# Moving an SBUF-to-SBUF transpose hop from the SyncE and ScalarE queues to GpSimd's queue

## The chip, the core and the metric

The kernel runs on one core of one Trainium2 chip. Five engines work from queues of their own: TensorE (PE), VectorE (DVE), ScalarE (ACT), GpSimd (POOL) and SyncE (SP). DMAs are begun by an instruction in the queue of SyncE, ScalarE or GpSimd and then carried by the core's 16 DMA engines. The metric is the device time of one execution, in microseconds; the median of two runs before the change is 1986.13 us (1984.96 to 1987.31).

## The reference

Two operators in a row, on an input of 8 batches x 3136 positions x 256 channels, float32:

```python
# 1: a filter along the sequence, by FFT
X = np.fft.rfft(x, axis=1)
Y = X * (filt_r + 1j * filt_i)[None]
x = np.fft.irfft(Y, n=x.shape[1], axis=1).astype(np.float32)
# 2: a gated feed-forward block
h = np.maximum(x @ w_in, 0.0)                      # 256 -> 1024
conv_out = sum(conv_w[k] * shifted(h, k) for k in range(3))   # along the sequence
out = (h * sigmoid(conv_out)) @ w_out              # 1024 -> 256
```

## The kernel before

The FFT of 3136 = 112 x 28 points is done as matrix products in stages. The first part of the kernel (the forward part, `NI` loop steps `i`) treats the eight batches as 8 x 14 = 112 pieces, each a pair of the 28 columns (`p` = 0 to 13). For a piece:

- `load` (L299): SyncE loads `x`, 112 partitions x 2 x 256 floats.
- `first` (L320): two matmuls with the table `s1` into a PSUM tile `ps`.
- `store_a` (L304): ScalarE copies `ps` to the SBUF tile `sa`.
- `turn` (L309), the hop: row 28r + g of `sa`, half j, goes to partition 14(2r + j) + p, place g, of the big tile `a_even` or `a_odd` (one for even batches, one for odd). What lay along partitions then lies along a row.
- `second` (L327): a matmul of one pair of columns of the whole `a` tile; it needs all 14 hops of its batch. Result in PSUM `pp`.
- `filt` (L337): three DVE products with the filter (`u`, and two halves of `v`), and on GpSimd z = u + v (L347).
- `third` (L349): two matmuls with `i1` into `ps`; `store_b` (L315): ScalarE copies to `sb` and begins the store to the DRAM tile `b_dram`.

In loop step `i` the order on each compute engine is as written: `load` for piece i+5, `filt` for i-18, `third` for i-20, `first` for i-1, `second` for i-17, the hop for i-2, then `store_b` and `store_a`. So hops are issued in steps 2 to 113, and the second stage begins in step 17. PE, ACT, DVE and POOL keep the written order (`manual_schedule`); SyncE's queue is put in order by a scheduler that knows what each DMA depends on. Between these, in the early steps, tables and filters are loaded, and the FFN weights, which come as 64-bit floats, are turned into 32-bit ones by DVE and GpSimd (`to_f32`, L157; `convert_weights`, L277; tile `ws`). Every engine's queue is served in order: an instruction that waits holds up all behind it.

The second part is the FFN (L428 on), with the last inverse stage of the next batch (`last_load`, `last_stage`, `last_out`, L199 to L225) put between its steps. The last stage of batch 0 runs in the last steps of the first part.

Number of buffers: `x` 7, `sa` 4, `sb` 4, `ws` 2. GpSimd's space for its DMA lists is `dynamic_dma_scratch_size=1024` bytes a partition. In each step the hop is eight DMAs of 28 rows of 1 KB, one for each half j and quarter r: six in SyncE's queue (`BY_SP = 6`), two in ScalarE's.

Of the kernel before, what the change touches and what calls it, by code (L numbers as in the profile page):

```python
# [9 lines left out]
F32 = mybir.dt.float32  # L10
# [10 lines left out]
D = 256  # L21
# [106 lines left out]
def tile_fft_filter_gated_ffn(  # L128
# [16 lines left out]
    nc = tc.nc  # L145
    B = x.shape[0]

    def hi_act(dst, src):
        nc.scalar.activation(dst, src, AF.Copy)  # L149
# [4 lines left out]
    def lo_pool(dst, src, hi):  # L154
        nc.gpsimd.tensor_tensor(out=dst, in0=src, in1=hi.bitcast(F32), op=ALU.subtract)  # L155

    def to_f32(dst, raw, e, m):  # L157


        v = nc.vector  # L160
        pairs = raw.rearrange("p (n t) -> p n t", t=2)
        low, high = pairs[:, :, 0].bitcast(U32), pairs[:, :, 1]
        v.tensor_scalar(e, high, 3, 0x3FFFFFF8, op0=ALU.logical_shift_left, op1=ALU.bitwise_and)
        yield
        v.tensor_scalar(m, high, 30, 30, op0=ALU.logical_shift_right, op1=ALU.logical_shift_left)
        yield
        v.tensor_tensor(out=e, in0=e, in1=m, op=ALU.bitwise_or)
        yield
        v.tensor_scalar(m, high, 27, 0xF, op0=ALU.logical_shift_right, op1=ALU.bitwise_and)
        yield  # L170
        v.scalar_tensor_tensor(out=dst, in0=m, scalar=7.0, in1=e.bitcast(F32), op0=ALU.is_ge, op1=ALU.mult)
        yield
        v.tensor_scalar(e, dst.bitcast(I32), 23, 23, op0=ALU.logical_shift_right, op1=ALU.logical_shift_left)
        yield
        v.scalar_tensor_tensor(out=e.bitcast(F32), in0=low, scalar=2.0**-52, in1=e.bitcast(F32), op0=ALU.mult, op1=ALU.mult)
        yield
        nc.gpsimd.tensor_tensor(out=dst, in0=dst, in1=e.bitcast(F32), op=ALU.add)
# [50 lines left out]
    xp = forward_pools.enter_context(tc.tile_pool(name="xp", bufs=2, side="right"))  # L228
    s1_sb = xp.tile([112, N2, 112], F32, name="s1_sb", bufs=1)
    a_sb = [xp.tile([112, G, D], F32, name="a_even", bufs=1)]  # L230
    with (
# [16 lines left out]
        rows = {}  # L248

        def load_filter(c):  # L250
            sl = slice(4 * c, 4 * c + 4)
            for t, src in ((t1_sb, fr), (t2_sb, fi)):
                nc.sync.dma_start(out=t[0:64, sl], in_=src[:, sl])
# [10 lines left out]
        def load_weights(k):  # L264
            raws[k] = raw = cv.tile([128, 2, 256], I32, name="raw")
            for part, src in enumerate((w_in, w_out)):
                nc.sync.dma_start(out=raw[:, part], in_=src[:, 256 * k:256 * k + 256])
# [9 lines left out]
        def convert_weights():  # L277

            for k in range(16):
                raw = raws.pop(k)  # L280
                em = cv.tile([128, 2, 256], I32, name="em", bufs=1)
                ws = cv.tile([128, 2, 128], F32, name="ws")
                yield from to_f32(ws.rearrange("p t n -> p (t n)"), raw.rearrange("p t n -> p (t n)"), em[:, 0], em[:, 1])
                yield
                parts = [[t.rearrange("p a b -> p (a b)")[:, 128 * k:128 * k + 128] for t in w] for w in (wi, wo)]
                for part, (wh, wl) in enumerate(parts):
                    hi_act(wh, ws[:, part])
                yield
                for part, (wh, wl) in enumerate(parts):
                    lo_pool(wl, ws[:, part], wh)  # L290
                    yield
                if k < 14:
                    load_weights(k + 2)
# [3 lines left out]
        psums = {}  # L297

        def load(b, p):  # L299
            r = xp.tile([112, 2, D], F32, name="x", bufs=7)  # L300
            nc.sync.dma_start(out=r, in_=x[b].rearrange("(p n) d -> p n d", n=N2)[:, 2 * p:2 * p + 2])
            rows["x", b, p] = r

        def store_a(b, p, ps):  # L304
            st = xp.tile([112, 2, D], F32, name="sa", bufs=4)
            nc.scalar.activation(st, ps, AF.Copy)  # L306
            rows["sa", b, p] = st

        def turn(engine, b, p, which):  # L309
            for q in which:  # L310
                j, r = divmod(q, 4)
                row = 14 * (2 * r + j) + p
                engine.dma_start(out=a_sb[b % 2][row:row + 1], in_=rows["sa", b, p][28 * r:28 * r + 28, j])  # L313

        def store_b(b, p, ps):  # L315
            st = fp.tile([112, 2, D], F32, name="sb", bufs=4)
            nc.scalar.activation(st, ps, AF.Copy)  # L317
            nc.scalar.dma_start(out=b_dram[b].rearrange("n (r g) d -> (n r) g d", g=G)[:, 2 * p:2 * p + 2], in_=st)

# [17 lines left out]
        def filt(b, p):  # L337


            pp, v = psums.pop((b, p)), turned[p % 2]  # L340
            sl = slice(2 * p, 2 * p + 2)
            u = fp.tile([120, 2, D], F32, name="u")
            nc.vector.tensor_mul(u, pp, t1_sb[:, sl])  # L343
            nc.vector.tensor_mul(v[64:120], pp[0:56], t2_sb[0:56, sl])  # L344
            nc.vector.tensor_mul(v[0:56], pp[64:120], t2_sb[64:120, sl])  # L345
            z = fp.tile([120, 2, D], F32, name="z", bufs=3)
            nc.gpsimd.tensor_tensor(out=z, in0=u, in1=v, op=ALU.add)  # L347
            parts["z", b, p] = z

        def third(b, p):  # L350
            z = parts.pop(("z", b, p))
            ps = fps.tile([112, 2, D], F32, name="ps")
            for j in range(2):
                nc.tensor.matmul(ps[:, j], lhsT=i1_sb[:, 2 * p + j], rhs=z[:, j], start=True, stop=True)  # L354
            return ps

        def at(i):
            return divmod(i, NP) if 0 <= i < NP * B else None
# [12 lines left out]
        with tc.manual_schedule(engines=COMPUTE):  # L371
            for i in range(NI):
                f, m = i, i - SKEW
                if i == done:
                    forward_pools.close()
                    yps.append(ctx.enter_context(tc.tile_pool(name="y_even", bufs=1, side="right", reuse_waits="tile")))
                    lp = ctx.enter_context(tc.tile_pool(name="lp", bufs=2, side="right", reuse_waits="tile"))
                if 1 <= i < 5:
                    nc.sync.dma_start(out=s1_sb[:, 4 * i + 8:4 * i + 12], in_=s1[:, 4 * i + 8:4 * i + 12])
                if (bp := at(f + 5)) and i:  # L380
                    load(*bp)
                if i == 6:
                    nc.sync.dma_start(out=s2_sb, in_=s2)
                    nc.sync.dma_start(out=s2s_sb, in_=s2s)
                    nc.sync.dma_start(out=m2_sb, in_=m2)
                if 12 <= i < 26 and i % 2 == 0:
                    sl = slice((i - 12) // 2 * 4, (i - 12) // 2 * 4 + 4)
                    load_filter(i // 2 - 6)
                    nc.sync.dma_start(out=i1_sb[:, sl], in_=i1[:, sl])
                if bp := at(m - 2):  # L390
                    filt(*bp)
                pt = third(*bp) if (bp := at(m - 4)) else None
                pf = first(*bp) if (bp := at(f - 1)) else None
                if bp := at(m - 1):
                    second(*bp)
                if bp := at(f - 2):
                    turn(nc.sync, *bp, range(BY_SP))
                    turn(nc.scalar, *bp, range(BY_SP, 8))
                    del rows["sa", bp[0], bp[1]]
                if pt is not None:  # L400
                    store_b(*at(m - 4), pt)
                if pf is not None:
                    store_a(*at(f - 1), pf)
                if 3 <= i < 16:
                    next(csteps, None)
                if i == 16:
                    load_weights(0)
                    load_weights(1)
                if i >= 22:
                    next(wsteps, None)  # L410
                    next(wsteps, None)
                if 16 <= i < 30 and i % 2 == 0:
                    copy_filter(i // 2 - 8)
                c = 2 * (i - done)
                if 0 <= c - 4 < N2:
                    last_out(0, c - 4)
                if 0 <= c - 2 < N2:
                    last_stage(0, c - 2, fps.tile([128, 512], F32, name="ps"))
                if 0 <= c < N2:
                    last_load(0, c)  # L420
# [107 lines left out]
                evacuate(*a)  # L528


BY_SP = 6
PLAG = 6
AVOID = (3, 4, 5, 6, 7)
COMPUTE = {mybir.EngineType.PE, mybir.EngineType.Activation, mybir.EngineType.DVE, mybir.EngineType.Pool}
# [38 lines left out]
```

## Time and profile before

| | us |
|---|---|
| median of the runs | 1986.13 |
| the profiled execution, its reported time | 1985.82 |
| its span, first to last instruction | 1983.9 |
| busy: PE / DVE / ACT / POOL | 1611.3 / 1322.9 / 1193.2 / 689.5 |
| forward part, to the first FFN matmul | 796 |
| FFN part | 1188 |
| mean granted TensorE clock | 0.891 |

In the profile, L313 is a line of the kernel before. SPq and ACTq are the DMA-issuing queues of SyncE and ScalarE; the time of an issue is the time in which that queue does nothing else. `a_even<-sa` is a DMA from `sa` to `a_even`. A group's row ends with the idle time before its instructions and who ended it. The reported time is 1.9 us more than the span.

### The profile page before, as it was taken

The numbers are of one execution on the slowest core, as the hardware profiler recorded it, in microseconds if no ns is written. First come the engines' busy times: TensorE is split into PE (matmuls) and PEld (weight loads), VectorE is DVE, ScalarE is ACT, GpSimd is POOL, SyncE is SP. The second block draws the span as 40 slices with busy tenths as digits, with TensorE's granted clock in tenths as the row PEclk, the third lists the DMA queues.
The fourth block names the chain that finished last, engine by engine and source line by source line (L and its number), as shares of the span: only waits on it lengthen the run. The fifth ranks groups of instructions, "written<-read, shape, count | busy, mean of one in ns | idle before, by whom it ended". The sixth has DMA issues, their size and how long they took to land.

```text
span 1983.9 us, 27237 instructions
## 1 busy us (share of the span) xinstructions
PE 1611.3 (81%) x9424; PEld 1382.6 (70%) x9424; DVE 1322.9 (67%) x2021; ACT 1193.2 (60%) x2178; POOL 689.5 (35%) x648
## 2 busy tenths in 40 slices
PE   4165647475645538999999999999999999999999
PEld 2032324243323326899999999999999999999998
DVE  0043526253544428788888888888888888888887
ACT  1122112121212114888888888888888888888887
POOL 0021313122212213344444444444444444444444
PEclk6576778676877769999999999999999999999999
DMA  4455444344444435011111111111111111110101
GB/s 122 99 136 138 109 112 114 105 120 111 121 109 118 105 89 155 29 43 53 37 43 44 47 43 48 42 43 43 47 43 44 46 42 43 48 42 21 37 19 38
DMA packets 127005, 141.22 MB, mean 71 GB/s; under 512 B 19899, under 2 KB 100884, under 8 KB 126868
## 3 DMA queue, kind: packets, MB, share of 16 engines
q1 hardware_dynamic: 103123, 107.35, 19.2%
q10 hardware_dynamic: 23744, 32.13, 6.1%
q8 instruction: 75, 1.23, 0.3%
q14 instruction: 63, 0.51, 0.1%
HBM read 62.34 MB, written 51.38 MB: 57 GB/s over the span
## 4 chain that ended last, share of the span: by engine, by line
PE 59%; DVE 2%; SPq 1%; DMA 1%; ACT 1%; issue 1%; ACTq 0%; POOL 0%; DVEq 0%; POOLq 0%
PE ps_h L181 9%; PE ps_h L182 9%; PE ps_h L180 9%; PE po L479 9%; PE po L481 9%; PE po L480 9%; PE ps_h L218 4%; SPq L313 1%; DVE y L152 1%; DMA a_odd<-sa 1%; ACT y L149 0%; DVE v L344 0%; DVE u L343 0%; PE ps L354 0%; PE pp L331 0%
## 5 line engine op out<-in xcount | busy, mean ns | idle before, releaser
L155 POOL TENSOR_TENSOR g<-t,g 128x448 fp32r<-128x448 f32 x448 | 517.3, 1155 | 667.8 <-ACT g L149 264.1
L479 PE MATMUL po<-wo,g 128*128 128x256 f32 x1568 | 441.5, 282 | 0.0
L481 PE MATMUL po<-wo,g 128*128 128x256 f32 x1568 | 433.8, 277 | 0.0
L480 PE MATMUL po<-wo,g 128*128 128x256 f32 x1568 | 433.4, 276 | 0.0
L453 DVE SCALAR_TENSOR_TENSOR t<-ps_h,cw,t 128x448 f32<-128x448 f32 x448 | 305.7, 682 | 83.3 <-ACT t L448 73.0
L343 DVE TENSOR_TENSOR u<-pp,t_sb 120x512 f32<-120x512 f32 x112 | 77.5, 692 | 417.6 <-PE pp L331 325.7
L181 PE MATMUL ps_h<-y,wi 128*128 128x450 f32 x896 | 330.7, 369 | 4.2 <-DVE y L152 4.2
L180 PE MATMUL ps_h<-y,wi 128*128 128x450 f32 x896 | 329.2, 367 | 3.5 <-ACT y L149 2.1
L182 PE MATMUL ps_h<-y,wi 128*128 128x450 f32 x896 | 329.0, 367 | 0.0
L454 DVE SCALAR_TENSOR_TENSOR t<-ps_h,cw,t 128x448 f32<-128x448 f32 x448 | 306.5, 684 | 16.0
L448 ACT ACTIVATE t<-ps_h,cw 128x448 f32<-128x448 f32 x448 | 284.8, 636 | 42.9 <-ACT ps_h L446 2.2
L347 POOL TENSOR_TENSOR z<-u,v 120x512 f32<-120x512 f32 x112 | 145.5, 1301 | 449.2 <-DVE v L345 382.9
L306 ACT ACTIVATE sa<-ps 112x512 f32<-112x512 f32 x112 | 66.9, 597 | 389.6 <-DMA a_even<-sa 174.3
L479 PEld LDWEIGHTS po<-wo,g 128*128 128x128 f32 x1568 | 294.8, 188 | 7.1
L480 PEld LDWEIGHTS po<-wo,g 128*128 128x128 f32 x1568 | 294.3, 188 | 5.7
L481 PEld LDWEIGHTS po<-wo,g 128*128 128x128 f32 x1568 | 294.5, 188 | 0.0
L459 DVE TENSOR_TENSOR t<-ps_h,t 128x448 f32<-128x448 f32 x448 | 275.4, 615 | 0.1
L446 ACT ACTIVATE ps_h<-ps_h 128x450 f32<-128x450 f32 x448 | 251.8, 562 | 32.1 <-PE ps_h L182 27.5
L458 ACT ACTIVATE t<-t 128x448 f32<-128x448 f32 x448 | 255.0, 569 | 11.9 <-DVE t L454 10.8
L149 ACT ACTIVATE g<-t 128x448 fp32r<-128x448 f32 x448 | 254.7, 568 | 0.2 <-DVE t L459 0.2
L324 PE MATMUL ps<-x,s_sb 112*112 112x256 f32 x448 | 162.9, 502 | 86.7 <-ACT sb L317 41.7
L354 PE MATMUL ps<-z,i_sb 120*112 120x256 f32 x448 | 145.9, 456 | 94.8 <-ACT sa L306 51.7
(57 smaller groups left out, 1776.8 us busy)
## 6 DMA issues: line engine op xcount, KB each, us to landing
x<-in_x SPq DMA_DIRECT2D x112, 224.0 KB
b_dram<-sb ACTq DMA_DIRECT2D x112, 224.0 KB
br<-b_dram SPq DMA_DIRECT2D x112, 224.0 KB
out<-ot SPq DMA_DIRECT2D x27, 896.0 KB
a_even<-sa SPq DMA_DIRECT2D x336, 28.0 KB
a_odd<-sa SPq DMA_DIRECT2D x336, 28.0 KB
a_even<-sa ACTq DMA_DIRECT2D x112, 28.0 KB
a_odd<-sa ACTq DMA_DIRECT2D x112, 28.0 KB
```

The lines of the kernel that those rows point to most:

```text
L155: nc.gpsimd.tensor_tensor(out=dst, in0=src, in1=hi.bitcast(F32), op=ALU.subtract)
L180: nc.tensor.matmul(ps, lhsT=wh, rhs=rh, start=start, stop=False, **kw)
L181: nc.tensor.matmul(ps, lhsT=wh, rhs=rl, start=False, stop=False, **kw)
L182: nc.tensor.matmul(ps, lhsT=wl, rhs=rh, start=False, stop=stop, **kw)
L448: nc.scalar.activation(t, h[:, 1:SUB + 1], AF.Copy, scale=cw[:, 1, f:f + 1])
L453: nc.vector.scalar_tensor_tensor(out=t, in0=h[:, 0:SUB], scalar=cw[:, 0, f:f + 1], in1=t, op0=ALU.mult, op1=ALU.add)
L454: nc.vector.scalar_tensor_tensor(out=t, in0=h[:, 2:SUB + 2], scalar=cw[:, 2, f:f + 1], in1=t, op0=ALU.mult, op1=ALU.add)
L458: nc.scalar.activation(t, t, AF.Sigmoid)
L459: nc.vector.tensor_mul(t, h[:, 1:SUB + 1], t)
L479: nc.tensor.matmul(o, lhsT=gh[:, sl], rhs=wo[0][:, f], start=first, stop=False, skip_group_check=True)
L480: nc.tensor.matmul(o, lhsT=gh[:, sl], rhs=wo[1][:, f], start=False, stop=False, skip_group_check=True)
L481: nc.tensor.matmul(o, lhsT=gl[:, sl], rhs=wo[0][:, f], start=False, stop=last, skip_group_check=True)
```

## The change

The hop is begun by GpSimd, in the same place of the loop step, as two DMAs, one for each half j. Each takes all 112 rows of its half of `sa`; its destination is four partitions, 28 apart. To make room for GpSimd's DMA lists, which grow from 1024 to 8192 bytes a partition, `x` has 6 buffers, `sa` and `sb` 3, `ws` 1. The FFN's code is the same.

```diff
-                ws = cv.tile([128, 2, 128], F32, name="ws")
+                ws = cv.tile([128, 2, 128], F32, name="ws", bufs=1)
...
-            r = xp.tile([112, 2, D], F32, name="x", bufs=7)
+            r = xp.tile([112, 2, D], F32, name="x", bufs=6)
...
-            st = xp.tile([112, 2, D], F32, name="sa", bufs=4)
+            st = xp.tile([112, 2, D], F32, name="sa", bufs=3)
...
-        def turn(engine, b, p, which):
-            for q in which:
-                j, r = divmod(q, 4)
-                row = 14 * (2 * r + j) + p
-                engine.dma_start(out=a_sb[b % 2][row:row + 1], in_=rows["sa", b, p][28 * r:28 * r + 28, j])
+        def turn(b, p):
+            st = rows.pop(("sa", b, p))
+            for j in range(2):
+                nc.gpsimd.dma_start(out=a_sb[b % 2][14 * j + p:112:28], in_=st[:, j])
...
-            st = fp.tile([112, 2, D], F32, name="sb", bufs=4)
+            st = fp.tile([112, 2, D], F32, name="sb", bufs=3)
...
                 if bp := at(f - 2):
-                    turn(nc.sync, *bp, range(BY_SP))
-                    turn(nc.scalar, *bp, range(BY_SP, 8))
-                    del rows["sa", bp[0], bp[1]]
+                    turn(*bp)
...
-BY_SP = 6
...
-    nc = bacc.Bacc("TRN2", target_bir_lowering=False, num_devices=1, dynamic_dma_scratch_size=1024)
+    nc = bacc.Bacc("TRN2", target_bir_lowering=False, num_devices=1, dynamic_dma_scratch_size=8192)
```

GpSimd's queue in the forward part, some steps with z and the weight conversion (`ws`, `wi`, `wo`), before:

```order
L347 TENSOR_TENSOR z<-u,v_97 120x512
L177 TENSOR_TENSOR ws<-ws,em 128x256
L347 TENSOR_TENSOR z<-u,v_96 120x512
L155 TENSOR_TENSOR wi_73<-ws,wi_72 128x128
L347 TENSOR_TENSOR z<-u,v_97 120x512
```

and after, with what each instruction waits for (`DMASW` is the completion of an earlier GpSimd DMA), at the place where batch 2 begins to write `a_even` again:

```order
L346 TENSOR_TENSOR z<-u,v_96 120x512 [waits DVE_49,PE_49,Pool_49]
L312 DMA a_even<-sa 4x28x256 [waits DMASW0_49,PE_49,Activation_49]
L312 DMA a_even<-sa 4x28x256 [waits DMASW1_49]
L346 TENSOR_TENSOR z<-u,v_97 120x512 [waits DVE_49,Pool_49]
L312 DMA a_even<-sa 4x28x256 [waits DMASW2_49,Activation_49]
L312 DMA a_even<-sa 4x28x256 [waits DMASW3_49]
L177 TENSOR_TENSOR ws<-ws,em 128x256
```

Between two z there is now a pair of DMAs, the first of which waits for ScalarE's copy, and at a batch's edge also for PE.

SyncE's queue in steps with filter loads, before:

```order
L301 DMA x<-in_x 112x512
L253 DMA t_sb<-in_fr 64x1024
L253 DMA t_sb<-in_fi 64x1024
L389 DMA i_sb<-in_i 120x448
L313 DMA a_odd<-sa 1x28x256 x6
L301 DMA x<-in_x 112x512
```

and after, the same loads:

```order
L301 DMA x<-in_x 112x512 x2
L253 DMA t_sb<-in_fr 64x1024
L253 DMA t_sb<-in_fi 64x1024
L388 DMA i_sb<-in_i 120x448
L253 DMA t_sb<-in_fr 64x1024
```

The six hop rows a step are gone, and the filter loads stand together, in front of the x loads of later pieces.

## The prediction

> **What bounds the kernel now.** The page first: the span, the slices, and the chain that ended last.
>
> ```profile
> span 1983.9 us, 27237 instructions
> PE   4165647475645538999999999999999999999999
> PEclk6576778676877769999999999999999999999999
> GB/s 122 99 136 138 109 112 114 105 120 111 121 109 118 105 89 155 29 43 53 37 43 44 47 43 48 42 43 43 47 43 44 46 42 43 48 42 21 37 19 38
> PE 59%; DVE 2%; SPq 1%; DMA 1%; ACT 1%; issue 1%; ACTq 0%; POOL 0%; DVEq 0%; POOLq 0%
> ```
>
> Two stages: some 16 slices (16 x 49.6 = 794 us) in which TensorE is half busy at a granted clock of 0.5 to 0.8, and 24 in which it is full. The chain's 59% PE speaks of the second stage, which the change does not touch. So the first is cut up by the table of stretches (from the start to the first second-stage matmul, to the last hop's issue, to the first FFN matmul, to the end):
>
> ```profile
> core 0: us, PE busy (x) PEld busy (x) DVE busy (x) ACT busy (x) POOL busy (x), PEclk, DMA share, GB/s
> 0.00:105.00 105.00, 29.29 (x68) 16.95 (x68) 1.17 (x7) 13.63 (x21) 1.51 (x8) 0.58 0.45 110
> 105.00:744.00 639.00, 360.42 (x974) 204.23 (x974) 274.85 (x406) 132.47 (x235) 151.58 (x146) 0.74 0.44 115
> 744.00:796.00 52.00, 43.25 (x207) 31.02 (x207) 41.77 (x56) 23.62 (x30) 18.14 (x18) 0.93 0.51 152
> 796.00:1984.00 1188.00, 1178.37 (x8175) 1130.39 (x8175) 1005.08 (x1553) 1023.48 (x1892) 518.26 (x476) 1.00 0.13 41
> ```
>
> Hops are issued in loop steps 2 to 113, and the second stage begins in step 17, so the first stretch holds 17 steps and the second 97: 639/97 = 6.59 us a step. In such a step PE is busy 360.42/97 = 3.72 us (at full clock about 3.72 x 0.74 = 2.75), DVE 274.85/97 = 2.83, ACT 1.37, POOL 1.56. Nobody computes for 6.59 us. The DMA engines are not full either: a share of 0.44 at 115 GB/s puts them at 115/0.44 = 261 GB/s when full. What else takes time is SyncE's queue:
>
> ```profile
> L313 SPq DMA_DIRECT2D a_even<-sa x336: 741/756/1534, 9.0 to 657.9; - x168
> L313 ACTq DMA_DIRECT2D a_even<-sa x112: 763/765/2073, 6.8 to 637.6; - x112
> L301 SPq DMA_DIRECT2D x<-in_x x112: 312/369/638, 1.2 to 700.0; - x112
> L318 ACTq DMA_DIRECT2D b_dram<-sb x112: 310/314/744, 116.2 to 793.8; - x112
> ```
>
> Columns: count, then shortest, median and longest issue in ns. A hop row of 28 pieces takes SyncE 0.756 us to begin, six a step are 4.5 us, and with the x load it is 4.9 us. The timeline of SyncE alone in mid-stage shows the rhythm:
>
> ```profile
> 447.32 4.89 SPq L313 DMA_DIRECT2D a_even<-sa  x6
> 452.31 0.47 SPq L301 DMA_DIRECT2D x<-in_x  x1
> 452.89 4.74 SPq L313 DMA_DIRECT2D a_even<-sa  x6
> 458.62 0.32 SPq L301 DMA_DIRECT2D x<-in_x  x1
> 459.04 4.75 SPq L313 DMA_DIRECT2D a_even<-sa  x6
> ```
>
> Six issues, about 1 us of nothing, the x load, six issues: 5.6 and 6.15 us between starts. The waits, SyncE's own and then ScalarE's, in 105 to 744, say what the gap is and who suffers:
>
> ```profile
> SPq L301 <- DMA a_odd<-sa: 24.2, 27, 2.0
> SPq L301 <- DMA a_even<-sa: 17.1, 19, 1.9
> ACT sa L306 <- DMA a_odd<-sa: 157.9, 47, 6.0
> ACT sa L306 <- DMA a_even<-sa: 120.9, 37, 5.2
> ```
>
> The x load waits 0.9 us a time (41.3 over 46) until a hop has landed, since both share completion semaphores; ScalarE waits 278.8 us for `sa` buffers that the hop has not yet read. At the stage's end SyncE stands alone on the chain:
>
> ```profile
> 743.21 0.76 SPq L313
> 744.00 2.76 DMA a_odd<-sa
> 746.86 2.03 PE pp L331 x2
> ```
>
> That the other engines can go faster when SyncE's delay is out of the way shows in a catch-up behind a batch's edge (timeline of PE):
>
> ```profile
> 308.37 1.03 PE L354 MATMUL ps<-z,i_sb 120*112 120x256 f32 x4
> 309.24 1.03 PE L324 MATMUL ps<-x,s_sb 112*112 112x256 f32 x4
> 310.10 1.02 PE L331 MATMUL pp<-a_even,s_sb 112*120 112x512 f32 x2
> 310.96 1.03 PE L354 MATMUL ps<-z,i_sb 120*112 120x256 f32 x4
> ```
>
> A whole step there takes 310.96 - 308.37 = 2.59 us.
>
> **The change part by part.** *Removed:* 672 SyncE issues and 224 ScalarE issues. SyncE keeps 0.37 us a step and the loads of tables and weights; ScalarE's queue loses 2 x 0.765 = 1.5 us a step and keeps 1.37 us of work and one 0.31 us issue. Neither can then hold a step of 2.6 us or more. The x load no longer shares semaphores with the hop. What is late next is on GpSimd.
>
> *Added:* 224 issues on GpSimd, two a step, each of 112 pieces. Its other work in 105 to 744:
>
> ```profile
> L347 POOL TENSOR_TENSOR z<-u,v 120x512 f32<-120x512 f32 x98 | 127.5, 1303 | 397.7 <-DVE v L345 363.1 <-PE ps L324 16.1 <-PE ps L354 8.8
> L177 POOL TENSOR_TENSOR ws<-ws,em 128x256 f32<-128x256 f32 x16 | 11.5, 721 | 0.0
> ```
>
> GpSimd works through z, hop, hop in written order, so its step is 1.56 + 2D + about 0.2 us for waits between instructions, D being one issue. No row of before shows a GpSimd issue. The lower bound of D is the 112-row store that ScalarE begins in 0.31 us; the upper, four issues of 28 pieces, which is the same 112 pieces: 4 x 0.756 = 3.02 us. Below zero is excluded: GpSimd issued no DMA before. I take 1.2 us: the geometric middle of the ends is 0.97, and the nearest row of GpSimd itself is its 1.30 us pass over z. Step: 1.56 + 2.4 + 0.2 = 4.16 us. The Trainium skill (DMA: Bandwidth & Descriptors, Latency and other measured facts) gives about 1 us to the first byte of a DMA begun by GpSimd against 0.6 from the other queues; with D = 1.0 the sum below would be 1682 instead of 1720. No run here shows it.
>
> *Waits added.* Two rows of the page price what stands around the hop, ScalarE's copy to `sa` and the first of three like products on DVE:
>
> ```profile
> L306 ACT ACTIVATE sa<-ps 112x512 f32<-112x512 f32 x112 | 66.9, 597 | 389.6 <-DMA a_even<-sa 174.3
> L343 DVE TENSOR_TENSOR u<-pp,t_sb 120x512 f32<-120x512 f32 x112 | 77.5, 692 | 417.6 <-PE pp L331 325.7
> ```
>
> A hop pair waits for ScalarE's `sa` of its step, and in the first step of a batch for the second-stage matmul that last reads this `a` tile. Behind it on GpSimd stands the next z, for which PE's third stage waits. `sa` is written a step ahead, so I cost this at nothing; the batch's edge has two GpSimd steps (8 us) between the last hop and the z that needs it, against 2.76 us of landing, one PE matmul and 3 x 0.69 = 2.1 us of DVE. If that cover is gone it costs some 3 us at each of 8 edges, 24 us.
>
> *Buffers:* `sa` 4 to 3: the loop is ScalarE 0.6, the hop pair 2.4, landing 2.8, a z in the way 1.3: 7.1 us over three steps, 2.4 a step, under 4.16. `sb` 4 to 3: 0.6 + 0.31 + landing of about 3 is under three steps too. `x` 7 to 6: still loaded six steps ahead. `ws` 2 to 1: the next DVE write comes two steps after the last GpSimd read; nothing, or at worst 16 waits of a hop pair, 38 us.
>
> *DMA engines:* a step moves x, the store and the hop:
>
> ```profile
> x<-in_x SPq DMA_DIRECT2D x112, 224.0 KB
> b_dram<-sb ACTq DMA_DIRECT2D x112, 224.0 KB
> a_even<-sa SPq DMA_DIRECT2D x336, 28.0 KB
> ```
>
> 3 x 224 KB (229 thousand bytes each) = 0.688 MB, at 261 GB/s 2.64 us. Under 4.16, so hidden. The Trainium skill says (same page, Issuing engines are not separate DMA queues) that DMAs of all queues run on the same 16 engines, so that another issuing engine saves only sequencer time, usually small beside the transfer. The trace disagrees with "small": 4.5 us of issue against 2.64 us of transfer. By that rule nothing would be won, the last rival but one.
>
> *Sum, for the profiled execution (span 1983.9, reported time 1985.8, the median 0.3 above that).* Head: it moves 105 x 110 GB/s = 11.6 MB; at the busiest slice's 155 GB/s that is 75 us (44 at 261). SyncE's order now puts the filter loads in front of later x loads, which is a reason not to go below 75. Middle: 97 x 4.16 = 403. Drain, 52: no hops in it, DVE busy 41.77, unchanged. FFN: 1188. Together 75 + 403 + 52 + 1188 = 1718, and 2 outside the span: 1720. As a formula: 1488 + 194 D.
>
> **The rivals.**
>
> *GpSimd is cheap, and PE and DVE set the pace.* D under 0.9. For it: the 0.31 us row. The step is then between 2.83 (DVE) and 3.72 (PE at 0.74), the clock rising with the load: 3.2 gives 75 + 310 + 52 + 1188 + 2 = 1627.
>
> *The hop crowds on four engines.* The Trainium skill (same page, Why a DMA increments its semaphore by 16 and not by 1) has the number of engines be the largest up to 16 that divides both sides' slowest dimension; the destination now has 4 rows. As a mechanism of this kernel: if all hops fell on the same four engines, at 261/16 = 16.3 GB/s each they carry 229/4 = 57 KB plus 2 x 229/16 = 29 KB a step, 86 KB in 5.3 us; 75 + 97 x 5.3 + 52 + 1188 + 2 = 1831. Against it: nothing says that it must be the same four.
>
> *No gain.* The issue is only swapped: D between 2.36 and 2.77 makes 1488 + 194 D fall within 2% (40 us) of 1986, which is about what a measurement of this kernel can tell from no change. It takes an issue 1.8 times as long as GpSimd's dearest row of the stage, z.
>
> *Slower.* GpSimd lists pieces at SyncE's price for 28, D = 3.02. Step 1.56 + 6.05 + 0.2 = 7.8 us; the head 17 x 6.05 = 103; 103 + 757 + 52 + 1188 + 2 = 2102. It decides from D = 2.57 on. For it: the four rows of the destination differ from the flat store that takes 0.31. Against: 0.756 us for 28 pieces and 0.31 for 112 show that on these queues the number of pieces does not set the price.
>
> That the change is not made as described is out: the order has two GpSimd rows where SyncE and ScalarE had eight.
>
> **How the numbers follow.** Forecast (D 0.9 to 1.8, 1663 to 1837): 0.60. Cheap GpSimd (1600 to 1663): 0.16. Four engines: 0.08. A dear issue with a small gain left (1850 to 1946): 0.03. No gain: 0.06. Slower: 0.07. So faster 0.87, same 0.06, slower 0.07. The range 1625 to 1850 holds the forecast, most of the cheap case and the four engines: about 0.82.
>
> **What would show it.** On the profile after: issues of L312 on GpSimd's queue, their median D; the step, as the hops' stretch over 97; ScalarE's waits for `sa` below 100 us; SyncE idle. Right if GpSimd's queue is nearly full at 4 us a step and PE's third stage waits for z. Wrong in the price if D lies outside 0.9 to 1.8; wrong in the mechanism if GpSimd has idle time and the step is still above 4 us: then landing, the buffers or the DMA engines hold it.

## The result and the profile after

The changed kernel takes 1686.44 us (median of two runs, 1684.36 to 1688.53) against 1986.13 us: a ratio of 0.849, 95% interval 0.844 to 0.854. The page of its profiled execution, first lines, slices and chain:

```profile
span 1686.4 us, 26441 instructions
PE   5288776877789999999999999999999999999999
PEclk7599889989899999999999999999999999999999
PE 76%; DMA 11%; DVE 5%; POOL 4%; issue 3%; ACT 1%; POOLq 0%; ACTq 0%; SPq 0%; DVEq 0%
```

The forward part has shrunk from 16 slices of 49.6 us to under 12 of 42.2 us. The shares of this chain add up to 100%, so it goes back to the start; those of the chain before add up to 65%, so it reached back to about 700 us only, and the shares of the two can't be compared one by one. In the chain now DMA landings are 11%, and no SyncE issue is left. The table of stretches, cut at the same four events as before (first second-stage matmul, last hop, first FFN matmul, end):

```profile
core 0: us, PE busy (x) PEld busy (x) DVE busy (x) ACT busy (x) POOL busy (x), PEclk, DMA share, GB/s
0.00:81.50 81.50, 28.25 (x68) 17.34 (x69) 1.26 (x7) 12.51 (x20) 22.93 (x40) 0.61 1.05 193
81.50:441.90 360.40, 285.45 (x975) 177.63 (x973) 294.42 (x405) 125.20 (x236) 275.12 (x337) 0.91 0.78 190
441.90:498.30 56.40, 43.83 (x207) 31.34 (x207) 41.84 (x58) 24.73 (x32) 21.23 (x21) 0.91 0.52 149
498.30:1686.40 1188.10, 1177.89 (x8176) 1129.83 (x8176) 1005.45 (x1553) 1023.59 (x1892) 518.30 (x476) 1.00 0.13 41
```

Against before (cut to the same tenths: 105.3, 638.7, 51.2, 1188.7): 24 us less in the head, 278 us less in the middle, 5 more in the drain, the FFN as it was. A step of the middle takes 360.4/97 = 3.72 us instead of 6.58. PE, DVE and GpSimd are each busy for 76 to 82% of it, at a granted clock of 0.91, and the DMA engines' share is 0.78 where it was 0.44.

The hop's issues on GpSimd, with the time from an issue to its landing, from the view of the tile `a_even`:

```profile
L312 POOL DMA_DIRECT2D a_even<-sa x112: 672/674/811, 7.2 to 391.7; - x112
DMA to landing us min/median/max: 3.7/7.2/14.5
```

An issue of 112 pieces takes 0.674 us. But the data land 7.2 us after the issue begins, some 6.5 after it ends, where before a hop on the chain landed 2.8 to 3.3 us after its issue had ended. The waits in the middle stretch:

```profile
ACT sa L306 <- DMA a_odd<-sa: 83.2, 31, 5.9
PEld ps L353 <- POOL z L346: 77.6, 68, 1.9
ACT sa L306 <- DMA a_even<-sa: 66.5, 32, 4.8
POOL z L346 <- DVE v L344: 64.6, 36, 6.4
```

ScalarE's wait for `sa` has about halved (149.7 us from 278.8), and in the other rows GpSimd waits for DVE and PE for GpSimd. The chain between 180 and 240 us shows a whole batch:

```profile
181.75 2.03 PE pp L330 x2
...
196.32 9.39 DMA a_odd<-sa
...
217.14 10.55 DMA a_odd<-sa
...
229.37 7.43 DMA a_odd<-sa
...
236.94 2.03 PE pp L330 x2
```

Two landings, of 9.39 and 10.55 us, end at ScalarE's next copy to `sa`. The last hop of the batch lands 7.43 us after its issue, and then PE begins the second stage with that batch. The first z of the batch follows at 241.3. At all seven edges between batches the first z starts 4.6 to 4.9 us after the landing of that batch's last hop. This is the time of the second-stage product (2.03 us) and three DVE products (2.1 us), with little between. So the landing of the last hop sets the edge. Where a step goes can be seen from the starts of the 112 z on GpSimd: inside a batch the mean interval is 3.40 us (before 4.82), at the seven edges between batches 8.1 us (before 24.8).

### The profile page after: what moved, and what is told of

The parts are those of the page before. It is cut to its first block, busy times and chain, and to the rows that moved or that the text cites. A ratio compares the mean times of both kernels' runs of the same rounds, so it can differ in the third digit from the quotient of the medians.

```text
span 1686.4 us, 26441 instructions
## 1 busy us (share of the span) xinstructions
PE 1535.4 (91%) x9424; PEld 1356.1 (80%) x9424; DVE 1343.0 (80%) x2021; ACT 1186.0 (70%) x2178; POOL 837.6 (50%) x872
## 3 DMA queue, kind: packets, MB, share of 16 engines
q8 instruction: 75, 1.23, 0.3%
## 4 chain that ended last, share of the span: by engine, by line
PE 76%; DMA 11%; DVE 5%; POOL 4%; issue 3%; ACT 1%; POOLq 0%; ACTq 0%; SPq 0%; DVEq 0%
PE ps_h L181 11%; PE ps_h L182 11%; PE ps_h L180 11%; PE po L476 11%; PE po L478 10%; PE po L477 10%; DMA a_odd<-sa 5%; PE ps_h L218 5%; PE pp L330 3%; PE ps L353 2%; PE ps L323 2%; POOL z L346 2%; DMA x<-in_x 1%; DVE v L343 1%; DMA a_even<-sa 1%
## 5 line engine op out<-in xcount | busy, mean ns | idle before, releaser
L478 PEld LDWEIGHTS po<-wo,g 128*128 128x128 f32 x1568 | 294.4, 188 | 0.0
L323 PE MATMUL ps<-x,s_sb 112*112 112x256 f32 x448 | 132.8, 427 | 54.8 <-DMA x<-in_x 46.4
L180 PEld LDWEIGHTS ps_h<-y,wi 128*128 128x128 f32 x896 | 170.0, 190 | 12.3 <-ACT y L149 3.3
L182 PEld LDWEIGHTS ps_h<-y,wi 128*128 128x128 f32 x896 | 168.3, 188 | 13.9
```

The costliest lines, as they stand in the source:

```text
L180: nc.tensor.matmul(ps, lhsT=wh, rhs=rh, start=start, stop=False, **kw)
L182: nc.tensor.matmul(ps, lhsT=wl, rhs=rh, start=False, stop=stop, **kw)
L478: nc.tensor.matmul(o, lhsT=gl[:, sl], rhs=wo[0][:, f], start=False, stop=last, skip_group_check=True)
```

## The experiments

The kernels `pool28`, `half_x` and `dve2` were run once, so differences of under 1% are not read from their times; of the other kernels the time is the median of four executions (of two for before and changed), which lie within 0.9%. For each run, worked out from its trace as above: when the second stage begins, the step of the middle (its length over 97), the mean interval between z inside batches 1 to 6 and at the seven edges, the median landing of hops to `a_even` and `a_odd` (the traces give it for GpSimd's DMAs), and the DMA share in the middle.

| run | time, us | 2nd stage from | step | inside | edge | landing | DMA share |
|---|---|---|---|---|---|---|---|
| before | 1986.1 | 105.3 | 6.58 | 4.82 | 24.8 | | 0.44 |
| changed | 1686.4 | 81.5 | 3.72 | 3.40 | 8.1 | 7.2, 6.5 | 0.78 |
| sp112 | 1755.2 | 75.5 | 4.45 | 3.47 | 12.9 | | 0.58 |
| bufs_only | 1976.1 | 108.0 | 6.47 | 4.99 | 20.8 | | 0.45 |
| pool28 | 1897.1 | 109.5 | 5.63 | 5.61 | 5.5 | 3.2, 3.0 | 0.50 |
| scr1024 | 1807.7 | 100.3 | 4.78 | 4.79 | 4.8 | 4.2, 4.1 | 0.55 |
| scr4096 | 1687.6 | 83.0 | 3.70 | 3.40 | 7.8 | 7.2, 6.1 | 0.77 |
| sa6_scr2k | 1694.3 | 84.3 | 3.81 | 3.67 | 6.3 | 6.8, 5.8 | 0.73 |
| sa5_scr4k | 1690.2 | 64.3 | 3.79 | 3.34 | 8.3 | 7.7, 7.3 | 0.81 |
| half_x | 1664.4 | 77.8 | 3.49 | 3.36 | 5.7 | 5.5, 5.0 | 0.65 |
| dve2 | 1678.4 | 84.4 | 3.65 | 3.45 | 6.6 | 8.1, 6.9 | 0.77 |
| turn_first | 1707.1 | 81.2 | 3.84 | 3.85 | 4.8 | 7.5, 6.8 | 0.72 |
| sp_pool | 1698.6 | 71.3 | 3.89 | 3.24 | 8.9 | 6.8, 6.5 | 0.71 |
| sp_pool_sa5 | 1719.1 | 72.7 | 4.07 | 3.29 | 11.3 | 6.5, 6.3 | 0.67 |

Two questions. Which part of the change brought the 300 us: two DMAs for eight, GpSimd's queue, the room for its lists? And what holds the step at 3.72 us, when GpSimd is idle for a quarter of it?

### Two DMAs of 112 rows, but from SyncE

```diff
-                nc.gpsimd.dma_start(out=a_sb[b % 2][14 * j + p:112:28], in_=st[:, j])
+                nc.sync.dma_start(out=a_sb[b % 2][14 * j + p:112:28], in_=st[:, j])
```

> The changed kernel with its two hop DMAs of 112 rows begun by SyncE instead of GpSimd; buffers as in the changed kernel. Theory A (the gain is GpSimd's: SyncE pays for a hop of this shape by its rows): an issue costs SyncE about 4 x 0.756 = 3.0 us, two a step 6.1 us, the step stays above 6 us, the time near 1986. Theory B (the gain is that of two issues instead of eight, whoever begins them): an issue of 0.3 to 0.8 us on SyncE, 0.6 to 1.6 us a step, and the time within 3% of the changed kernel's 1686. Theory C (the hop of four destination rows crowds on four DMA engines when begun by SyncE): cheap issue, but landing above 10 us and a step of 5 us or more, 1800 or more.

1755.22 us, ratio 0.885 (0.883 to 0.887). The issue row and SyncE's longest waits in the middle:

```profile
L312 SPq DMA_DIRECT2D a_even<-sa x112: 625/632/2017, 8.5 to 454.5; - x112
SPq L301 <- DMA b_dram<-sb: 69.4, 26, 4.9
SPq L312 <- DMA a_odd<-sa: 39.6, 39, 2.7
SPq L312 <- DMA a_even<-sa: 33.4, 35, 1.6
SPq L312 <- DMA b_dram<-sb: 31.3, 8, 7.6
```

SyncE issues the 112 rows in 0.632 us, less than it took for 28 (0.756). Theories A and C fall, and B holds in its mechanism, though not to its 3%: 229 us of the 298 are there without GpSimd, with two DMAs where eight were issued (8 of them come with the smaller buffers, next section). The run also takes ScalarE's two issues away, and none separates these from SyncE's six. GpSimd adds the other 69. Those are not the issue time, since 0.632 and 0.674 are alike, and hardly the round inside a batch (3.47 against 3.40, 5 us in all). They lie in the first batch, in which z goes from its first to its 14th start in 79.1 us instead of 45.4 (34 us), and at the seven edges (12.9 against 8.1, 33 us); the head is 6 us shorter. SyncE, which also loads x and the filters, stands 174 us in the four waits shown, for landings of hops and of ScalarE's stores. That the 69 us come from what stands late behind these waits is likely, but no run takes these waits away alone.

### The smaller buffer counts alone

```diff
-                ws = cv.tile([128, 2, 128], F32, name="ws")
+                ws = cv.tile([128, 2, 128], F32, name="ws", bufs=1)
...
-            r = xp.tile([112, 2, D], F32, name="x", bufs=7)
+            r = xp.tile([112, 2, D], F32, name="x", bufs=6)
...
-            st = xp.tile([112, 2, D], F32, name="sa", bufs=4)
+            st = xp.tile([112, 2, D], F32, name="sa", bufs=3)
...
-            st = fp.tile([112, 2, D], F32, name="sb", bufs=4)
+            st = fp.tile([112, 2, D], F32, name="sb", bufs=3)
```

(on the kernel before)

> The kernel before with only the buffer counts of the change (x 6, sa 3, sb 3, ws 1). As forecast the smaller counts cost nothing by themselves: 1986 within 0.5%. The rival (ScalarE waits longer for sa, of which one buffer less is there): the loop of sa through ScalarE's copy 0.6, issue 4.7 and landing 3 takes 8.3 us plus queueing over three steps instead of four; if it binds, the step grows by up to a tenth, 2040 to 2050.

1976.08 us, ratio 0.996 (0.994 to 0.997): 8 us less, not more. ScalarE does wait longer for `sa` (299.2 us in the middle, from 278.8), but inside a step that SyncE sets. Why it is a little shorter is not known; the edges are 4 us shorter (20.8) and the steps inside 0.17 longer.

### Eight DMAs of 28 rows, from GpSimd

```diff
-                nc.gpsimd.dma_start(out=a_sb[b % 2][14 * j + p:112:28], in_=st[:, j])
+                for r in range(4):
+                    row = 14 * (2 * r + j) + p
+                    nc.gpsimd.dma_start(out=a_sb[b % 2][row:row + 1], in_=st[28 * r:28 * r + 28, j])
```

> The changed kernel with GpSimd beginning the eight DMAs of 28 rows a step. If an issue on GpSimd costs by the DMA (0.67 us whatever its rows), GpSimd is busy 1.5 + 8 x 0.67 = 6.9 us a step and the time is 1960 to 2020. If it costs by the row (0.67/4 = 0.17 us), GpSimd is busy as in the changed kernel, and the time is 1650 to 1700.

1897.08 us. The issue row, and the middle stretch (109.5 to 655.1):

```profile
L314 POOL DMA_DIRECT2D a_even<-sa x448: 505/505/666, 7.1 to 577.0; - x150
109.50:655.10 545.60, 362.97 (x974) 215.41 (x974) 293.33 (x406) 128.17 (x236) 529.57 (x924) 0.80 0.50 127
```

Between the two expectations. An issue on GpSimd costs 0.505 us for 28 pieces and 0.674 for 112; a straight line through the two gives an estimate of 0.45 us fixed and 2 ns a piece (0.169/84), mostly the DMA and hardly the pieces. And here GpSimd does set the pace: it is busy 529.57 of 545.60 us, and 8 x 0.505 + 1.56 = 5.60 us is the interval inside a batch, 5.61. So the prediction's model of GpSimd's queue is right when that queue is the bound (its 0.2 us for waits left out). The batch's edge costs nothing here: hops land in 3.1 us, and at six of the seven edges z starts 7.6 to 9.7 us after the last landing, so it is not the landing that it waits for.

Four kernels with the small buffers make a square. Two DMAs for eight are worth 221 us from SyncE and ScalarE (1976 to 1755) and 211 from GpSimd (1897 to 1686). GpSimd in place of the other queues is worth 79 us with eight DMAs and 69 with two.

### The room for GpSimd's DMA lists

```diff
-    nc = bacc.Bacc("TRN2", target_bir_lowering=False, num_devices=1, dynamic_dma_scratch_size=8192)
+    nc = bacc.Bacc("TRN2", target_bir_lowering=False, num_devices=1, dynamic_dma_scratch_size=1024)
```

> The changed kernel with GpSimd's space for DMA lists put back to 1024 bytes a partition, buffers as in the changed kernel. If the larger space matters (issues wait for room), GpSimd's issue grows from 0.67 to 2 us or more and the time to 1750 or above. If not, 1686 within 0.5%, and the buffers were given up for nothing.

1807.72 us, ratio 0.911 (0.909 to 0.912), 121 us more than the changed kernel. An issue takes its 0.68 us as before; the time is lost ahead of it, 91.5 us in the stretch from 110 to 440. GpSimd in mid-stage (start, length, idle before and what ended it):

```profile
303.55 0.70 POOL L312 DMA_DIRECT2D a_even<-sa  x1 [0.44 <-issue]
304.87 0.67 POOL L312 DMA_DIRECT2D a_even<-sa  x1 [0.62 <-issue]
...
307.65 0.70 POOL L312 DMA_DIRECT2D a_even<-sa  x1 [0.41 <-issue]
310.13 0.67 POOL L312 DMA_DIRECT2D a_even<-sa  x1 [1.77 <-issue]
```

"issue" is a wait for nothing that the profile shows. It is gone with more room, all else equal:

```diff
-    nc = bacc.Bacc("TRN2", target_bir_lowering=False, num_devices=1, dynamic_dma_scratch_size=8192)
+    nc = bacc.Bacc("TRN2", target_bir_lowering=False, num_devices=1, dynamic_dma_scratch_size=4096)
```

> The changed kernel with 4096 bytes for GpSimd's DMA lists. With 1024 bytes GpSimd stands still about 1 us ahead of a hop DMA and the time is 1808; with 2048 (and 6 sa buffers) it does so in a third of them, 1694. If the room needed is that of the hops in flight (7 us of landing at two hops a 3.7 us step, some four hops), 4096 bytes hold them: GpSimd has no such idle time and the time is 1686 within 0.7%. If 8192 is needed, 1690 to 1720 with such idle time.

1687.57 us, ratio 0.850 (0.848 to 0.852), the changed kernel's time. So the room is worth 121 us, and half of what the change took is enough.

### More buffers for `sa`

```diff
-            st = xp.tile([112, 2, D], F32, name="sa", bufs=3)
+            st = xp.tile([112, 2, D], F32, name="sa", bufs=6)
```

(with 2048 bytes for the lists)

> The changed kernel with 6 sa buffers instead of 3 (space for DMA lists 2048 bytes). Theory A (the step of 3.72 us is the loop of three sa buffers through a hop that lands in 7 us): the loop is spread over six steps, ScalarE's wait for sa falls from 150 us in the stage to below 50, the step to 3.1 to 3.3 us, the next bounds being DVE 294.5/97 = 3.04 and GpSimd 2.84: 1625 to 1650. Theory B (the DMA engines have no more to give): more hops in flight land later, the step stays within 2% of 3.72, 1670 to 1690.

1694.31 us. The run does not decide: `sa` waits fell to 17.5 us, but GpSimd stood 33 us ahead of hops in the stretch from 110 to 440, as with 1024 bytes, though less. Hence the same with 5 buffers and 4096 bytes:

> The same with 5 sa buffers. Theory A (the loop of sa buffers through a hop that lands in 7 us holds the step): against the run with 4096 bytes and 3 buffers ScalarE's wait for sa falls by half or more and the time by 20 to 45 us. Theory B (the step inside a batch, 3.4 us, is held by the round of DVE, GpSimd and PE at their own work, the rest by the batch's edge): the wait for sa falls, the time by less than 10 us.

1690.17 us, ratio 0.850 (0.847 to 0.853), against 1687.57 with three buffers. ScalarE's waits for the hop in the middle:

```profile
ACT sa L306 <- DMA a_odd<-sa: 10.3, 7, 2.1
ACT sa L306 <- DMA a_even<-sa: 5.6, 4, 2.1
```

They fall from 147 us with three buffers to 16, and the time does not move. Theory A, that the loop of `sa` buffers alone holds the step, falls. The chain shown above did run through this wait; with it gone the step inside a batch is 3.34 us instead of 3.40, so something else holds it nearly as long, and hops land later (7.7 and 7.3 us). Taking away 130 us of waits on ScalarE gained nothing.

### Half of the x loads

```diff
+            if p % 2 and (b, p) != (0, 1):
+                rows["x", b, p] = rows["x", b, p - 1]
+                return
             r = xp.tile([112, 2, D], F32, name="x", bufs=6)
...
-            r = rows.pop(("x", b, p))
+            r = rows["x", b, p]
```

> The changed kernel, loading x for every second piece only and using it for two pieces (so half of the input is left out). It takes 0.115 MB from the 0.69 MB that a step moves. If the DMA engines' load makes the hop's landing slow (7 us, where it took 3 before), landing falls to 5 us or less, ScalarE's wait for sa falls by more than half, and the step goes from 3.72 to about 3.2 us: 1635 or less. If the landing is the hop's own length, it stays near 7 us and the time within 1% of 1686.

1664.43 us. With the DMA share at 0.65 instead of 0.78 a hop lands in 5.0 to 5.5 us. The step inside a batch is nearly unchanged (3.36 against 3.40). The edges are 2.5 us shorter: 7 x 2.5 = 17 us of the 21.5 by which the middle is shorter. The last hop of a batch lands 4.8 us after the end of its issue (mean of the seven edges) instead of 6.8, which is 2.0 of the 2.5 us. So landing, slower the more the DMA engines carry, costs at the batch's edge; inside a batch no cost shows. The expectation had it in every step.

### One DVE product less

```diff
-            nc.vector.tensor_mul(v[0:56], pp[64:120], t2_sb[64:120, sl])
+            if b == 0 and p < 2:
+                nc.vector.tensor_mul(v[0:56], pp[64:120], t2_sb[64:120, sl])
```

> The changed kernel without the third of the three DVE products of a filter step (the lower half of v keeps the values of the first two pieces). DVE is busy 294.5 us of the stage's 361, 0.69 us of each step's 3.04 go. If DVE sets the step, 97 x 0.69 = 67 us go: 1620. If the hop's landing or the DMA engines set it, less than a third of that: 1665 to 1686.

1678.35 us, 8 less where 67 would have gone. The mean step inside a batch did not get shorter (3.45). DVE, with 82% the busiest engine, does not set it by itself. Place by place there is more to see: the second to fourth z intervals of a batch fell by 0.2 to 0.4 us (to 3.15, 3.09 and 3.23), and some of the later ones grew by as much or more (the 12th from 3.10 to 4.30), so DVE takes part behind the edge, and something else after it. Hops landed later here, 8.1 and 6.9 us.

### The hop ahead of z

```diff
+                if bp := at(f - 2):
+                    turn(*bp)
                 if bp := at(m - 2):
                     filt(*bp)
...
-                if bp := at(f - 2):
-                    turn(*bp)
```

> The changed kernel with the hop pair written ahead of z in each loop step. Theory A (landing of the hop sets the step, also at the batch's edge): each hop starts up to a z pass (1.3 us) earlier, a loop of three steps gets 1.3 us shorter, 0.2 to 0.4 us a step: 1645 to 1670. Theory B (z is the late one, PE's third stage waits for it): z starts behind two issues, 1690 to 1720.

1707.12 us, ratio 0.860 (0.858 to 0.863). In this kernel the first hop of a batch overwrites the `a` tile before the last pair of the batch two before is read, so that pair is computed from other data, and its matmul waits for that hop: the interval at the last place of a batch grew to 9.25 us and that at the edge fell to 4.8. The run moved a wait and does not tell whether z or landing is late.

### One half from each queue

```diff
-                nc.gpsimd.dma_start(out=a_sb[b % 2][14 * j + p:112:28], in_=st[:, j])
+                (nc.gpsimd, nc.sync)[j].dma_start(out=a_sb[b % 2][14 * j + p:112:28], in_=st[:, j])
```

> One of the two 112-row hop DMAs of a step from GpSimd, the other from SyncE. GpSimd's own time a step falls from 2.84 to 2.16 us, SyncE's rises by 0.63. If GpSimd's queue holds the step inside a batch (3.4 us), it falls to about 3.0 (DVE) and the time to 1640 to 1660. If landing or the DMA engines hold it, no gain: 1680 to 1700. If SyncE's copy of the hop is late by itself (the run with both on SyncE took 1755), between the two: 1700 to 1730.

1698.62 us, ratio 0.855 (0.853 to 0.856), 12 us more than the changed kernel. GpSimd is busy 211 us of the middle instead of 275, and the interval inside a batch falls by 0.16 to 3.24 us. But the first batch loses more: z goes from its first to its 15th start in 77.4 us instead of 48.6. SyncE again has filter loads behind hops there, which is the likely reason. With 5 buffers and 4096 bytes:

> The same with 5 sa buffers and 4096 bytes for GpSimd's lists, which now hold half as many hops. If GpSimd's queue and the sa loop both take part, this is the shortest of all: 1625 to 1650. If the batch's edge and the DMA engines hold the stage, it is within 10 us of the run without it.

1719.09 us, ratio 0.866 (0.864 to 0.868). Slower still, with edges of 11.3 us; no run here separates why five buffers cost in this kernel what they did not cost in the other. No version that does the whole work beats the changed kernel; `scr4096` ties with it.

## Why the prediction was right, and where it was not

The direction and the range hold (1686 in 1625 to 1850), and the point was 34 us too high. But the forecast's own case did not happen: it rested on an issue of 0.9 to 1.8 us, and the measured one is 0.674; and GpSimd's queue, which was to be nearly full, is idle for 24% of the middle. That the point came so near is in part luck: two errors offset each other. With the measured issue the formula gives 1619 us. The middle took 59 us more than its sum says, the head 6.5 and the drain 4.4, which makes 1689; the profiled execution took 1688.5.

*What bounds the kernel: right.* The issues of the eight DMAs set the step. With two issues in place of eight, SyncE alone gives 229 us (sp112), and the smaller buffers alone nothing that costs (bufs_only). What the prediction did not see is where the time lay: it divided 639 us by 97 steps, but before the interval was 4.82 us inside a batch and 24.8 at an edge. Of the 278 us that the middle lost, 7 x 16.6 = 116 were at the edges.

*D, the price of an issue: mis-sized, 1.2 us taken, 0.674 measured.* In the formula 1488 + 194 D that is 194 x 0.526 = 102 us too slow. The upper bound (four times SyncE's price for 28 pieces) was far off, since the price is mostly per DMA on GpSimd (0.505 for 28, 0.674 for 112) as on SyncE (0.756 for 28, 0.632 for 112). The prediction had noted from SyncE's and ScalarE's rows that pieces do not set the price, and yet used it for nothing but a rival. The figure of about 1 us to the first byte that the Trainium skill gives (DMA: Bandwidth & Descriptors, Latency and other measured facts) is no price of the queue. GpSimd's next instruction starts after 0.67 us, and the last bytes have landed after 7; no run here shows the first byte.

*The middle's sum: wrong.* With the measured D the sum of GpSimd's own work is 1.56 + 1.35 + 0.2 = 3.11 us a step; the step is 3.72. The missing 0.61 x 97 = 59 us have two parts. The batch's edge costs 8.1 - 3.4 = 4.7 us, seven times (there are seven edges, not eight), 33 us; "I cost this at nothing" is the failed step, with 24 us named for the case that its cover goes. Each side of its comparison was off. The last hop lands 6.8 us after the end of its issue (mean of the seven edges) and not 2.76. From there to z it is another 4.7 us, where a matmul and 2.1 us were reckoned. And the cover, two GpSimd steps, is 2 x 3.4 = 6.8 us and not 8. So 11.5 us stand against 6.8, and 4.7 are left, which is the edge's cost. With 1024 bytes of list space steps are 4.8 us and landings 4.1: the cover is there, and the edge, 4.8, costs nothing. The rest is the step inside a batch, 3.40 us against 3.11. No single resource sets it: taking 0.69 us from DVE, 0.68 from GpSimd, half the x traffic from the DMA engines, or the `sa` wait from ScalarE moved it by +0.05, -0.16, -0.04 and -0.06. With PE, DVE and GpSimd each busy 2.8 to 3.0 us of it, in-order queues that wait for one another are the likely cause; that is argued, and stays open.

*DMA engines hidden at 2.64 us a step: right for the throughput, wrong for the landing.* A step takes 0.78 x 3.72 = 2.90 us of them. At shares of 0.55, 0.65 and 0.78 a hop of 112 pieces lands in 4.1, 5.3 and 6.8 us (means of the medians for the two tiles; 28 pieces at 0.50 in 3.1): the faster the stage, the later each hop. The other rows of the table go the same way, but not strictly (7.1 at 0.72, 6.3 at 0.73). The Trainium skill's rule that all queues share the 16 engines (DMA: Bandwidth & Descriptors, Issuing engines are not separate DMA queues) agrees in this. Its remark there that the issue time saved is usually small beside the transfer does not fit here: before, SyncE spent 4.5 us of a 6.58 us step on issues, and with 1.3 in their place (sp112) the kernel took 229 us less.

*Head and drain.* The head took 81.5 us for the 75 forecast, moving 193 GB/s with the DMA engines full (share 1.05), and it moved 15.7 MB and not 11.6. How much of the loads falls into it differs between the kernels: with five `sa` buffers it moved 12.4 MB in 64.3 us, and the first batch took longer. The drain took 56.4 for 52.

*The rivals.* Cheap GpSimd was the case that came, with D under 0.9, but its pace of 3.2 us and 1627 us were missed for the same two reasons. The crowding on four engines did not show as a step of 5.3 us, and in sp112, where it was the third theory, the step inside a batch is 3.47. No gain and slower fell with D. The clock rose to 0.91, as the text of the cheap rival said.

*Waits for `sa` below 100 us* was a sign named in advance and did not come (149.7), and the run with five buffers shows that by itself it says nothing about the time.

## What to carry to other kernels

When a queue that only issues DMAs sets a stage's step, count its issues before asking who makes them: here six small ones take 4.5 us a step of SyncE's queue and eight take 4.0 of GpSimd's, and two large ones 1.3 of either. A queue of its own then helps in another place, here in the first batch and at the batch edges, most likely by what no longer stands behind its waits. And once a stage goes faster, recost every landing at the new load; a transfer that was hidden with 3 us may not be with 7, first of all where a whole group must have landed.

## What was not expected of the hardware

GpSimd stands still ahead of a DMA when its list space is small: 91.5 us in the stretch from 110 to 440 with 1024 bytes (121 us on the whole time), 33 in the same stretch with 2048 (and six `sa` buffers), 0.3 with 4096. The profile shows no releaser for it, only idle time marked "issue".

DVE's conversion of the weights can be held up by GpSimd. The DVE timeline of the changed kernel, while z ran from 309.98 to 311.28:

```profile
309.73 0.43 DVE L167 TENSOR_TENSOR em<-em 128x256 int32<-128x256 int32 x1
310.19 1.24 DVE L169 TENSOR_SCALAR em<-raw 128x256 int32<-128x256 int32 x1
```

Beside z it matters which of the two began first. L169 and L173, two instructions of the same shape, took 1.23 to 1.25 us nine times when they began while z was running, and ended 0.15 us after z. Seven times they had begun 0.15 us ahead of z, and took 0.29 to 0.30 us. Before, it was the same: 1.24 us beside a running z, 0.294 otherwise.

The making of a DMA list can hold DVE too. L165, again of this shape, began four times 0.2 us into the first of a hop's two issues and took 1.35 us, to 0.2 us past the end of the second, with no z running. Three L169 that began 0.07 us into an issue, 0.6 us ahead of z, took 2.05 us, to past the end of z. Yet at other places beside an issue it took 0.294 to 0.304 us, and what decides is not known. The conversion adds the 20 us of busy DVE to the middle (294.4 from 274.9), 9.6 of them in L165.
